# Linear attention with top-1 experts on one core: state sums, tables, a weight load and three copies in another order

## The chip, the core and the metric

One core of a Trainium2 chip runs the whole program. Its engines are TensorE (PE, with PEld for its weight loads), VectorE (DVE), ScalarE (ACT), GpSimd (POOL) and SyncE (SP, which issues most transfers). The metric is the device time of one execution in microseconds. Three timed runs of the kernel before gave 348.38, 348.40 and 348.96 us, median 348.4.

## The reference

```python
# attention: B, H, S, D = 4, 8, 768, 48
for t in range(S):
    state = alpha[:, :, t, :, None] * state + einsum('bhd,bhe->bhde', k[:, :, t], v[:, :, t])
    y[:, :, t] = einsum('bhd,bhde->bhe', q[:, :, t], state)
x = y.transpose(0, 2, 1, 3).reshape(B * S, H * D)          # 3072 rows of 384
# experts: E = 8, F = 1024
logits = x @ w_gate + modality_bias[modality_id]
e_idx = argmax(logits, axis=1)
gate_w = softmax(logits)[arange(N), e_idx]
for e in range(E):
    mask = e_idx == e
    out[mask] = gate_w[mask, None] * (maximum(x[mask] @ w1[e], 0) @ w2[e])
```

## The kernel before, in words

**Attention.** The four batches make two groups of two, and each sequence six chunks of 128 tokens, so there are 12 pairs (`PS`), numbered 0 to 11; pair s holds 256 rows of x. A loop over steps s works as a pipeline: step s scans alpha for the pairs s and s+1, computes scores and outputs of pair s-1, and turns, stores and routes pair s-2. For each pair and each half z of its heads (z0, z1), DVE scans alpha backwards (`G`, in `back`) and forwards (`Fw`, in `forth`); the keys are scaled by G on POOL (`kh`), the queries by Fw on DVE or POOL (`qh`). PE makes the scores from kh and qh, ACT copies them out (`scT`), POOL sets the acausal half to zero, PE multiplies with v. The state is carried from pair to pair: PE sums keys times values in the PSUM tile `kv` (`states`), DVE adds what came before to S (`state`: `S<-UB,kv`), POOL scales S by the decay (`decayed`: `UB<-S,G`), and PE multiplies the queries with UB at the next step (`from_state`: `b<-qh,UB`). Of every six pairs the first needs no UB.

**Routing.** PE multiplies the outputs with the gate's weights (`logits_turned`, copied to `lts` by ACT) and adds their four parts with `fold` (`add_logits`: `kv<-fold,lts`, in the same PSUM tile as kv). DVE finds the expert of each row (`route_group`, last result `oh`), PE counts, DVE turns counts into ranks and places (`rank_...`, `route_places`, `keys_early`). The sorted rows go in slots of 256 to the experts. The first two slots are chosen early, from the rows known so far: expert number to `meta`, weights by SP (`weights`), rows by two indirect transfers of POOL (`gather`: `xg<-xd,idx`).

**Experts.** From about 120 us PE works through 11 full slots and a half one: layer 1 with w1, layer 2 with w2, each weight split into a high and a low part (`w1H`, `w1L`). The first slot uses w2 as it was loaded (`y<-w2r,hf`).

**What sets the order.** The wrapper `Ordered` keeps PE, DVE, ACT and POOL in the order of the code; `at(s, phase, f)` puts a routing step at a place in the pipeline. A transfer of SP is placed by a scheduler unless `tc.issue_after` ties it to an instruction. Each engine works through its own list, and a waiting instruction holds all behind it.

Of the kernel before, what the change touches and what calls it, by code (L numbers as in the profile page):

```python
# [8 lines left out]
F32 = mybir.dt.float32  # L9
# [3 lines left out]
I32 = mybir.dt.int32  # L13
U32 = mybir.dt.uint32
ALU = mybir.AluOpType
AF = mybir.ActivationFunctionType
AX = mybir.AxisListType
# [4 lines left out]
P = 128  # L22
# [54 lines left out]
def attention_moe(ctx: ExitStack, tc: tile.TileContext, q, k, v, alpha, at_, kt_, qt_, vt_, mid, wg, wgp_, mb, w1, w2, out):  # L77
# [123 lines left out]
    of = cp.tile([P, DM], F32, name="of")  # L201
    pool.memset(of, 0.0)
    ti = ac.tile([P, NU], I32, name="ti")
    pool.iota(ti, [[P, NU]], base=-MID, channel_multiplier=1)
    tok = cp.tile([P, NU], F32, name="tok")
    pool.tensor_copy(tok, ti)
    tge = ac.tile([P, NU], F32, name="tge")
    pool.tensor_scalar(tge, tok, 0.0, None, op0=ALU.is_ge)
    pool.tensor_tensor(tok, tok, tge, op=ALU.add)
    rev = cp.tile([P, E], F32, name="rev")  # L210
    ones = cp.tile([P, P], BF16, name="ones")
    tri = cp.tile([P, P], BF16, name="tri")
# [46 lines left out]
    def scaled_queries(s, z, engine=vec):  # L259
        engine.tensor_tensor(st[s, "q"][:, z], QT[s % NB][:, z], seg(st[s, "F"], 1, z), op=ALU.mult)  # L260
# [49 lines left out]
    def decayed(s):  # L310
        if s % NC > 0:
            A = st[s, "G"][:, 1::SEG].unsqueeze(2).broadcast_to([P, KS, D])
            pool.tensor_tensor(UB[s % 2][:, :, :D], st[s, "S"], A, op=ALU.mult)

    def from_state(s):
        yk = [bank(NP, P) for _ in range(2)]
        st[s, "yp"] = yk
        st[s, "fresh"] = {(z, x) for z in range(2) for x in range(2)}
        if s % NC > 0:
            qh, U = st[s, "q"], UB[s % 2]  # L320
            for j in range(NP):
                for z in range(2):
                    for g in range(2):
                        x = g ^ z
                        k = NP * z + j
                        pe.matmul(yof(yk, z, x, j), U[halves[g], k], qh[halves[g], k], start=new(s, z, x), stop=False)
# [25 lines left out]
    def state(s):  # L352
        if s % NC > 0:
            S1 = sb.tile([P, KS, D], F32, name="S")
            kv = st[s - 1, "kv"]
            if s % NC > 1:
                vec.tensor_tensor(S1, UB[(s - 1) % 2][:, :, :D], kv, op=ALU.add)
            else:
                vec.tensor_copy(S1, kv)
            st[s, "S"] = S1  # L360
# [13 lines left out]
                        stop=(j == NP - 1),  # L374
                    )

    def outputs(s):
        yt = sb.tile([P, 2, NP, P], F32, name="yt")
        for z in range(2):
            act.copy(yt[:, z], st[s, "yp"][z])  # L380
        st[s, "yt"] = yt

    def rows(s):
        xs = sb.tile([P, 2, DM], F32, name="xs")
# [159 lines left out]
    K8 = cp.tile([P, E], F32, name="K8")  # L544
    K16 = cp.tile([P, 2, E], F32, name="K16")
    zi = ac.tile([P, 1], I32, name="zi")
    zc = cp.tile([P, 1], F32, name="zc")
    sz = cp.tile([P, 1], F32, name="sz")
    dz = cp.tile([P, NH], F32, name="dz")

    def counting_tables():
        pool.tensor_scalar(rev, iof[:, :E], -1.0, float(E), op0=ALU.mult, op1=ALU.add)
        pool.memset(ones, 1.0)
        for u in range(2):
            pool.tensor_scalar(thr0[:, u], iof[:, :NS0], float(T), float(P * u), op0=ALU.mult, op1=ALU.add)
        pool.memset(on16, 1.0)
        pool.memset(beg[:, 0:1], 0.0)
        pool.memset(C[:, 0:1], 0.0)
        pool.tensor_scalar(K8, rev, -float(NU), None, op0=ALU.mult)
        pool.memset(dE, 1.0)  # L560
        pool.memset(dE[:, 0:1], 0.0)
        pool.memset(dE[:, E : E + 1], 1.0 - E)

    def token_tables():
        pool.affine_select(tri, ones, [[1, P]], ALU.is_gt, 0.0, base=0, channel_multiplier=-1)
        pool.tensor_copy(tok16, tok)
        pool.iota(zi, [[0, 1]], base=0, channel_multiplier=1)
        pool.tensor_copy(zc, zi)
        pool.tensor_scalar(dz, ident[:, :NH], zc, None, op0=ALU.mult)
# [5 lines left out]
    hi = cp.tile([P, NU], F16, name="hi")  # L575
    OH = cp.tile([P, NU, NH], F16, name="OH")
    def half_index():

        hz = cp.tile([P, NS], F32, name="hz")
        vec.tensor_scalar(hz, iof[:, 1 : NS + 1], 2.0, None, op0=ALU.mult)  # L580
        vec.tensor_scalar(hz, hz, zc, None, op0=ALU.is_le)
        vec.tensor_reduce(sz, hz, axis=AX.X, op=ALU.add)

    def places(tp, z):
        return vec.tensor_scalar(idx[:, z], tp, float(MID), 0.0, op0=ALU.add, op1=ALU.max)
# [279 lines left out]
    def at(s, phase, f, *a):  # L865
        later.setdefault((s, phase), []).append((f, a))

    def run(s, phase):
        for f, a in later.pop((s, phase), ()):
            f(*a)  # L870

    for m in range(NM + 1):
        at(3 + m, "masks", bias_table, m)
    at(6, "end", token_tables)
    at(7, "end", half_index)
    at(7, "end", route_group, 0, 10)
    at(8, "small", rank_counts, 0, 10)
    at(8, "middle", rank_masks, 0, 10)
    at(8, "middle", rank_sums, 0, 10)
    at(8, "end", rank_split, 0, 10)  # L880
    at(9, "middle", route_places, 0, 5)
    at(9, "sums", route_places, 5, 10)
    at(9, "end", route_group, 10, 16)
    at(10, "small", rank_counts, 10, 16)
# [1 line left out]
    at(10, "middle", rank_sums, 10, 16)  # L886
    at(10, "sums", count_early, 0)
    at(10, "sums", choose_early, 0)
    at(10, "end", rank_split, 10, 16)
    at(10, "end", route_places, 10, 16)  # L890
    at(10, "end", keys_early, 0)
    at(11, "small", early_places, 0)
    at(11, "small", gather, 0, row(EARLY[0]))
    at(11, "end", gate_values, 0, EARLY[0])

    ZS = (Z0, Z1)
    MORE, LESS = (4,), (11,)
# [18 lines left out]
    def warm(n):  # L916
        w = bank(NP, P)
        for i in range(n):
            pe.matmul(w[:, i % NP], ident, ident, start=True, stop=True)

    for s in range(PS):
        if 0 < s and s + 1 < PS:
            load(s + 1, "kqv")
        if 0 <= s - 2:
            outputs(s - 2)
        late, by = [], vec
        if s == 0:
            warm(14)
            begin(0)
            for z in ZS:  # L930
                back(0, z)
                scaled_keys(0, z, pool)
                totals(0, z)
                forth(0, z)
                scaled_queries(0, z, vec if z == Z0 else pool)
                if z == Z0:
                    counting_tables()
        elif s == 1:
            begin(1)
            scores(0, 0)  # L940
            for z in range(2):
                turn_keys(0, z)
                warm(4)
            back(1, Z0)
            scaled_keys(1, Z0, pool)
            scores(0, 1)
            totals(1, Z0)
            forth(1, Z0)
            scaled_queries(1, Z0, pool)
            back(1, Z1)  # L950
            scaled_keys(1, Z1, pool)
            totals(1, Z1)
            forth(1, Z1)
            scaled_queries(1, Z1)
        else:
            state(s - 1)
            decayed(s - 1)
            for z in range(2):
                scores(s - 1, z)
            run(s, "masks")  # L960
            todo = scans(s)
            if len(todo) > 1:
                late = todo.pop()
            if s >= 4:
                by = pool
            for f in todo:
                do(f)
            run(s, "counts")
        if 1 < s:
            keys(s - 1)  # L970
        if 0 <= s - 2:
            rows(s - 2)
        if 0 <= 2 * (s - 3) < TURNED:
            turn_logits(s - 3)
        if 0 <= s - 2:
            logits_turned(s - 2)
        run(s, "small")
        if 0 <= 2 * (s - 3) < TURNED:
            sum_logits(s - 3)
        run(s, "middle")  # L980
        do(late[:-1])
        if 0 <= s - 1:
            from_state(s - 1)
        if TURNED <= 2 * (s - 2):
            add_logits(s - 2)
        if 0 <= s - 1:
            states(s - 1)
        run(s, "sums")
        for f, *x in late[-1:]:
            f(*x, by)  # L990
        if 0 <= s - 1:
            from_values(s - 1)
        run(s, "end")
        for c in range(s - (s < 5), s + 1 - (s < 4)):
            if 0 <= c < PS:
                guard(c)
        if 0 <= s - 2:
            store(s - 2)
        for c in range(s + 2 + (s > 4), s + 3 + (s > 3)):
            if c < PS:  # L1000
                load(c, "a")
        if s == 2:
            sp.dma_start(xd[MID : MID + 1], of[0:1])
            sp.dma_start(gd[MID : MID + 1], of[0:1, 0:1])
# [34 lines left out]
    def w1_part(i, j):  # L1039
        return split("w1", WR[i % 2][0][:, :, 256 * j : 256 * (j + 1)])  # L1040
# [18 lines left out]
    t = GROUPS[-2:]  # L1059
    state(l)  # L1060
    decayed(l)
    w1s = [w1_part(0, 0)]
    outputs(l - 1)
    for z in range(2):
        scores(l, z)
    out_of_range()
    rows(l - 1)
    logits_turned(l - 1)
    gate_rows(0, EARLY[0])
    gather_gates(0, row(EARLY[0]))  # L1070
    store(l - 1)
    weights(0, 0, (1,))
    from_state(l)
    add_logits(l - 1)
    prep(0, False)
# [3 lines left out]
    low_inputs(0)  # L1079
    rank_counts(*t[0])  # L1080
    count_early(1)
    choose_early(1)
    rank_masks(*t[0])
    w1s += [w1_part(0, 1)]
    outputs(l)
    hp = first_block(0, w1s[0], lambda: logits_turned(l), True)
    rank_split(*t[0])
    keys_early(1)
    w1s += [w1_part(0, 2)]
    rows(l)  # L1090
    store(l)
# [281 lines left out]
```

## Time and profile before

| | |
|---|---|
| median of three timed runs | 348.4 us |
| profiled execution | 349.39 us, its span 347.7 us |
| busy in the span: PE, PEld, DVE | 334.3, 303.0, 270.5 us |
| busy in the span: ACT, POOL | 229.8, 171.4 us |
| transfers | 76.53 MB, mean 220 GB/s |

The span runs from the first to the last instruction of the core; the execution's own time is 1.7 us longer. Shares of busy time are means over stages: the attention lasts until about 115 us, and the experts until 340 us. A gap on PE in either stage has a name, and the views say what ended it.

### The profile page before, as it was taken

The numbers are of one execution on the slowest core, as the hardware profiler recorded it, in microseconds if no ns is written. First come the engines' busy times: TensorE is split into PE (matmuls) and PEld (weight loads), VectorE is DVE, ScalarE is ACT, GpSimd is POOL, SyncE is SP. The second block draws the span as 40 slices with busy tenths as digits, with TensorE's granted clock in tenths as the row PEclk, the third lists the DMA queues.
The fourth block names the chain that finished last, engine by engine and source line by source line (L and its number), as shares of the span: only waits on it lengthen the run. The fifth ranks groups of instructions, "written<-read, shape, count | busy, mean of one in ns | idle before, by whom it ended". The sixth has DMA issues, their size and how long they took to land. (4 is left out here: it accounts for less than half of the span.)

```text
span 347.7 us, 8429 instructions
## 1 busy us (share of the span) xinstructions
PE 334.3 (96%) x3174; PEld 303.0 (87%) x3174; DVE 270.5 (78%) x486; ACT 229.8 (66%) x454; POOL 171.4 (49%) x185
## 2 busy tenths in 40 slices
PE   8999999999898999999999999999999999999991
PEld 8788888888786886898989898989898989898991
DVE  7999999899995768786868686868686868686530
ACT  1677978767566624777777777777777777777530
POOL 7978898787765225555242424232354342411021
PEclk9999999999999999999999999999999999999998
DMA  7999999999169292997776667667586776770010
GB/s 243 393 303 261 244 244 249 252 248 228 48 207 342 101 353 74 378 380 265 255 244 207 246 210 247 206 226 232 180 268 227 232 247 207 236 216 23 2 48 32
DMA packets 39369, 76.53 MB, mean 220 GB/s; under 512 B 4300, under 2 KB 20837, under 8 KB 39317
## 3 DMA queue, kind: packets, MB, share of 16 engines
q1 hardware_dynamic: 35220, 65.83, 61.1%
q0 software_dynamic: 4096, 10.05, 8.6%
q8 instruction: 27, 0.44, 0.5%
q14 instruction: 26, 0.20, 0.2%
HBM read 66.22 MB, written 9.65 MB: 218 GB/s over the span
## 5 line engine op out<-in xcount | busy, mean ns | idle before, releaser
L67 PE MATMUL b<-xHL,w1H 128*128 128x512 f32 (+1 forms) x312 | 103.2, 381 | 0.0
L67 POOL DMA_INDIRECT out_dram<-os,idx x25 | 27.4, 1096 | 112.2 <-ACT os L67 72.1
L67 PE MATMUL b<-xHL,w1L 128*128 128x256 f32 x288 | 80.7, 281 | 0.0
L67 PEld LDWEIGHTS b<-xHL,w1H 128*128 128x128 f32 x312 | 57.4, 188 | 11.8 <-issue 0.4
L67 PE MATMUL y<-w2H,hH 128*128 128x384 f32 x184 | 62.5, 340 | 0.0
L67 PE MATMUL y<-w2H,hL 128*128 128x384 f32 x184 | 61.6, 335 | 0.0
L67 PE MATMUL y<-w2L,hH 128*128 128x384 f32 x184 | 61.5, 334 | 0.0
L67 DVE TENSOR_TENSOR hs<-b,low 128x256 f32<-128x256 f32 x88 | 33.9, 416 | 32.8 <-ACT low L67 31.3
L67 PEld LDWEIGHTS b<-xHL,w1L 128*128 128x128 f32 x288 | 54.3, 189 | 0.1
L67 DVE TENSOR_TENSOR w1L<-w1r,w1H 128x768 fp32r<-128x768 f32 x48 | 43.9, 952 | 6.6 <-ACT w1H L67 6.6
L67 DVE TENSOR_TENSOR w2L<-w2r,w2H 128x768 fp32r<-128x768 f32 x48 | 45.9, 961 | 3.4 <-ACT w2H L67 3.1
L67 ACT ACTIVATE os<-y,gg 128x384 f32<-128x384 f32 x25 | 14.6, 582 | 39.9 <-PE y L67 39.9
L67 ACT COPY low<-b 128x256 f32<-128x256 f32 x88 | 30.4, 367 | 14.8 <-PE b L67 14.6
L67 ACT CAST w2H<-w2r 128x768 fp32r<-128x768 f32 x48 | 40.0, 841 | 0.0
L67 ACT CAST w1H<-w1r 128x768 fp32r<-128x768 f32 x48 | 37.9, 838 | 2.3 <-POOL kh L67 2.3
L67 POOL DMA_INDIRECT gg<-gd,idx x26 | 29.1, 1120 | 19.6 <-issue 13.3
L67 POOL DMA_INDIRECT xg<-xd,idx x26 | 27.6, 1061 | 19.3 <-DVE idx L67 9.8
L67 PEld LDWEIGHTS y<-w2L,hH 128*128 128x128 f32 x184 | 34.6, 188 | 0.0
L67 PEld LDWEIGHTS y<-w2H,hH 128*128 128x128 f32 x184 | 34.6, 188 | 0.0
L67 PEld LDWEIGHTS y<-w2H,hL 128*128 128x128 f32 x184 | 34.5, 188 | 0.0
L67 ACT COPY scT<-b 128x512 f32<-128x512 f32 x48 | 24.9, 598 | 14.2 <-PE b L67 14.0
L67 POOL TENSOR_TENSOR kh<-kt,G 128x512 f32<-128x512 f32 x24 | 31.7, 1328 | 5.2 <-DVE G L67 2.1
(176 smaller groups left out, 605.2 us busy)
## 6 DMA issues: line engine op xcount, KB each, us to landing
w1r<-in_w_dram SPq DMA_DIRECT2D x26, 768.0 KB
w2r<-in_w_dram SPq DMA_DIRECT2D x26, 768.0 KB
vt<-in_paired_v_dram SPq DMA_DIRECT2D x12, 384.0 KB
xd<-xs SPq DMA_DIRECT2D x12, 384.0 KB
X<-in_turned_alpha_dram SPq DMA_DIRECT2D x18, 193.7 KB
kt<-in_turned_k_dram SPq DMA_DIRECT2D x18, 192.0 KB
qt<-in_turned_q_dram SPq DMA_DIRECT2D x18, 192.0 KB
kt<-in_turned_k_dram SPq DMA_DIRECT2D x4, 256.0 KB
```

The lines of the kernel that those rows point to most:

```text
L67: ins = f(*a, **kw)
```

## The change

Five things are done together.

- **State sums.** `state` of pair 9 runs in step 9 ahead of `route_places` and `route_group`, that of pair 10 in step 10 ahead of `rank_split`. In the last step, the gate's values (`gate_values`) come behind `state` and `decayed`. In the steps that start a sequence, `states` stands ahead of `add_logits`.
- **Transfers.** The load of the first slot's w2 is tied to the store of pair 10 (the last but one of the twelve).
- **Start.** The first query products change engines: z0 goes to POOL, z1 to DVE. Of eight filler matmuls (`warm`) in step 1 two stay.
- **Tables.** Constant tables on POOL move: the counting tables ahead of the first kh, the token tables to the end of step 8, the slot tables to the last step; `half_index` is two DVE instructions in place of three, and later.
- **Output copy.** One of the last pair's two copies on ACT (`yt`) goes ahead of a cast of w1.

On VectorE, in steps 9 and 10, around the routing of tiles 10 to 15: before,

```order
L67 SCALAR_TENSOR_TENSOR Fw<-X_87,room 128x516
L67 TENSOR_TENSOR OL<-ioh,lo 128x640
L67 TENSOR_TENSOR L<-kv,bt 128x48
L67 TENSOR_REDUCE mx<-L 128x6
L67 TENSOR_TENSOR ls<-L,mx 128x48
L67 SCALAR_TENSOR_TENSOR eq<-ls,rev 128x48
L67 TENSOR_REDUCE m_176<-eq 128x6
L67 TENSOR_TENSOR oh<-eq,m_176 128x48
L67 TENSOR_TENSOR S<-UB_138,kv 128x384
```

and of the change:

```order
L67 SCALAR_TENSOR_TENSOR Fw<-X_87,room 128x516
L67 TENSOR_TENSOR S<-UB_138,kv 128x384
L67 TENSOR_TENSOR OL<-ioh,lo 128x640
L67 TENSOR_TENSOR L<-kv,bt 128x48
L67 TENSOR_REDUCE mx<-L 128x6
L67 TENSOR_TENSOR ls<-L,mx 128x48
L67 SCALAR_TENSOR_TENSOR eq<-ls,rev 128x48
L67 TENSOR_REDUCE m_172<-eq 128x6
L67 TENSOR_TENSOR oh<-eq,m_172 128x48
```

The state sum S of pair 9 moves past seven routing instructions; oh, which PE counts, now stands behind it.

On SyncE's queue, from the first slot's w1 (`w1r_92`) on, with `xd<-xs` the stores of rows and `gd<-gs` the store of gates: before,

```order
L67 DMA w1r_92<-in_w_dram 128x3x512
L67 DMA xd<-xs 128x2x384
L67 TENSOR_LOAD meta
L67 ISA x3
L67 DMA w2r_93<-in_w_dram 128x4x384
L67 ISA
L67 DMA w2r_93<-in_w_dram 128x4x384
L67 DMA xd<-xs 128x2x384
L67 DMA gd<-gs_16_1942 16x128
L67 DMA xd<-xs 128x2x384
```

and of the change:

```order
L67 DMA w1r_92<-in_w_dram 128x3x512
L67 DMA xd<-xs 128x2x384 x2
L67 DMA gd<-gs_16_1932 16x128
L67 DMA xd<-xs 128x2x384
L67 TENSOR_LOAD meta
L67 ISA x3
L67 DMA w2r_93<-in_w_dram 128x4x384
L67 ISA
L67 DMA w2r_93<-in_w_dram 128x4x384
```

Both halves of w2 (`w2r_93`) now stand behind the stores of pairs 9 and 10 and the gates.

On GpSimd at the start, around the key products kh of pair 0: before,

```order
L67 TENSOR_SCALAR tge<-tok 128x24
L67 TENSOR_TENSOR tok<-tok,tge 128x24
L67 TENSOR_TENSOR kh<-kt_82,G 128x512
L67 TENSOR_SCALAR rev<-iof 128x8
L67 MEMSET ones 128x128
L67 TENSOR_SCALAR thr_199<-iof 128x12 x2
L67 MEMSET dE 128x16
L67 MEMSET dE 128x1 x2
L67 TENSOR_TENSOR kh<-kt_82,G 128x512
L67 TENSOR_TENSOR qh<-qt_84,Fw 128x512
```

and of the change:

```order
L67 TENSOR_SCALAR K_202<-rev 128x8
L67 MEMSET dE 128x16
L67 MEMSET dE 128x1 x2
L67 TENSOR_TENSOR kh<-kt_82,G 128x512
L67 TENSOR_TENSOR qh<-qt_84,Fw 128x512
L67 TENSOR_TENSOR kh<-kt_82,G 128x512
L67 AFFINE_SELECT scT<-scT 128x1024
```

POOL now has qh of z0 between the two kh, the tables stand ahead of both, and qh of z1 is gone from POOL.

The diff, without the moved table lines that repeat:

```diff
-    pool.iota(ti, [[P, NU]], base=-MID, channel_multiplier=1)
-    pool.tensor_copy(tok, ti)
-    pool.tensor_scalar(tge, tok, 0.0, None, op0=ALU.is_ge)
-    pool.tensor_tensor(tok, tok, tge, op=ALU.add)
...
-    def outputs(s):
+    def outputs(s, zs=(0, 1)):
...
-    def counting_tables():
-        pool.tensor_scalar(rev, iof[:, :E], -1.0, float(E), op0=ALU.mult, op1=ALU.add)
...
+    pool.tensor_scalar(rev, iof[:, :E], -1.0, float(E), op0=ALU.mult, op1=ALU.add)
+    pool.memset(ones, 1.0)
...
+    def order_table():
+        pool.affine_select(tri, ones, [[1, P]], ALU.is_gt, 0.0, base=0, channel_multiplier=-1)
+
+    def token_table():
+        pool.iota(ti, [[P, NU]], base=-MID, channel_multiplier=1)
+        pool.tensor_copy(tok, ti)
+        pool.tensor_scalar(tge, tok, 0.0, None, op0=ALU.is_ge)
+        pool.tensor_tensor(tok, tok, tge, op=ALU.add)
+        pool.tensor_copy(tok16, tok)
...
+    def slot_tables():
         for u in range(2):
             pool.tensor_scalar(thr0[:, u], iof[:, :NS0], float(T), float(P * u), op0=ALU.mult, op1=ALU.add)
...
-        vec.tensor_scalar(hz, iof[:, 1 : NS + 1], 2.0, None, op0=ALU.mult)
-        vec.tensor_scalar(hz, hz, zc, None, op0=ALU.is_le)
-        vec.tensor_reduce(sz, hz, axis=AX.X, op=ALU.add)
+        with nc.allow_low_precision("whole numbers"):
+            vec.tensor_scalar(zh, zi, 1, None, op0=ALU.arith_shift_right)
+        vec.tensor_scalar(sz, zh, float(NS), None, op0=ALU.min)
...
-    at(6, "end", token_tables)
-    at(7, "end", half_index)
+    at(6, "end", order_table)
+    at(8, "end", token_table)
...
+    at(9, "sums", state, 9)
     at(9, "sums", route_places, 5, 10)
...
+    at(10, "end", state, 10)
     at(10, "end", rank_split, 10, 16)
...
-    at(11, "end", gate_values, 0, EARLY[0])
...
-                scaled_queries(0, z, vec if z == Z0 else pool)
-                if z == Z0:
-                    counting_tables()
+                scaled_queries(0, z, pool if z == Z0 else vec)
...
-                warm(4)
+                if z == 0:
+                    warm(2)
...
-            state(s - 1)
+            if (s - 1, "S") not in st:
+                state(s - 1)
             decayed(s - 1)
+            run(s, "state")
...
+        if 0 <= s - 1 and (s - 1) % NC == 0:
+            states(s - 1)
         if TURNED <= 2 * (s - 2):
             add_logits(s - 2)
-        if 0 <= s - 1:
+        if 0 <= s - 1 and (s - 1) % NC:
             states(s - 1)
...
+    gate_values(0, EARLY[0])
     w1s = [w1_part(0, 0)]
...
+    slot_tables()
     out_of_range()
...
     store(l - 1)
-    weights(0, 0, (1,))
+    with tc.issue_after(sp.last):
+        weights(0, 0, (1,))
...
     count_early(1)
+    outputs(l, (0,))
     choose_early(1)
     rank_masks(*t[0])
     w1s += [w1_part(0, 1)]
-    outputs(l)
+    outputs(l, (1,))
...
     keys_early(1)
+    half_index()
```

## Rows read from the trace of the kernel before

**Rows 1.** Windows: engines' busy time, PEclk, DMA share, GB/s; and page part 2, PE

```profile
24.00:56.00 32.00, 32.00 (x572) 27.82 (x570) 31.09 (x41) 26.01 (x57) 27.35 (x28) 1.00 0.99 251
56.00:104.00 48.00, 45.78 (x801) 40.17 (x799) 45.76 (x83) 32.68 (x74) 36.12 (x35) 1.00 0.79 204
104.00:120.00 16.00, 14.35 (x189) 11.85 (x184) 9.72 (x39) 9.94 (x21) 7.29 (x7) 1.00 0.57 206
120.00:340.00 220.00, 220.00 (x1341) 203.43 (x1340) 163.07 (x297) 148.45 (x281) 78.84 (x72) 1.00 0.65 217
PE   8999999999898999999999999999999999999991
```

**Rows 2.** Waits of PE in 0 to 140 us: us in total, times, longest

```profile
PE b L67 <- POOL UB L67: 1.2, 2, 0.9
PE b L67 <- DMA xg<-xd,idx: 0.9, 2, 0.6
PE kv L67 <- ACT lts L67: 0.6, 1, 0.6
PE b L67 <- ACT yt L67: 0.6, 1, 0.6
...
PE b L67 <- DVE ohs L67: 0.3, 1, 0.3
```

**Rows 3.** Timeline of the start: start, duration, engine, operation, idle before and releaser

```profile
1.42 5.85 PE L67 MATMUL b<-ident 128*128 128x128 f32 x28 [1.42 <-POOL ident masks.py:199]
...
6.34 0.69 DVE L67 TENSOR_TENSOR qh<-qt,Fw 128x512 f32<-128x512 f32 x1
...
7.19 1.23 DVE L67 TENSOR_TENSOR_SCAN G<-X,room 128x516 f32<-128x516 f32 x1 [0.15 <-DMA X<-in_turned_alpha_dram]
...
9.98 1.19 POOL L67 TENSOR_TENSOR qh<-qt,Fw 128x512 f32<-128x512 f32 x1 [0.29 <-DVE Fw L67]
...
15.21 1.14 DVE L67 TENSOR_TENSOR qh<-qt,Fw 128x512 f32<-128x512 f32 x1
...
17.45 1.16 PE L67 MATMUL b<-qh,kh 48*128 48x128 f32 x16 [0.43 <-POOL kh L67]
```

**Rows 4.** Timeline of PE in step 7

```profile
62.69 0.61 PE L67 MATMUL kv<-fold,lts 128*128 128x8 f32 x4 [0.64 <-ACT lts L67]
63.23 1.14 PE L67 MATMUL kv<-vt,knat 128*64 128x48 f32 x32
```

**Rows 5.** Timeline of DVE at the end of step 7

```profile
64.39 1.12 DVE L67 TENSOR_SCALAR hz<-iof 128x19 f32<-128x19 f32 x1
65.62 1.03 DVE L67 TENSOR_SCALAR hz<-hz,zc 128x19 f32<-128x19 f32 x1
```

**Rows 6.** Timeline around the state of pair 9

```profile
88.27 0.21 DVE L67 TENSOR_TENSOR oh<-eq,m 128x48 bf16<-128x48 f32 x1
...
89.02 0.84 POOL L67 TENSOR_TENSOR UB<-S,G 128x384 f32<-128x384 f32 x1 [1.33 <-DVE S L67]
...
89.91 1.10 PE L67 MATMUL b<-qh,UB 64*64 64x128 f32 x32 [0.92 <-POOL UB L67]
```

**Rows 7.** Timeline around the state of pair 10

```profile
98.78 0.55 DVE L67 TENSOR_TENSOR S<-UB,kv 128x384 f32<-128x384 f32 x1
```

**Rows 8.** Timeline of w2's load, its first use and the gather; DMA queues, 104 to 108

```profile
99.57 1.09 SPq L67 DMA_DIRECT2D w2r<-in_w_dram  x2
...
104.11 1.26 POOL L67 DMA_INDIRECT xg<-xd,idx  x1 [0.17 <-DVE sm L67]
...
127.18 3.39 PE L67 MATMUL y<-w2r,hf 128*128 128x384 f32 x10
...
q1 hardware_dynamic: 1035, 1.54, 104.2%
```

**Rows 9.** Timeline of ACT, the last pair's second output copy

```profile
115.95 0.58 ACT L67 COPY yt<-b 128x512 f32<-128x512 f32 x1 [1.42 <-PE b L67]
```

**Rows 10.** Windows: the span's end

```profile
344.60:347.60 3.00, 0.00 (x0) 0.00 (x0) 0.00 (x0) 0.00 (x0) 0.00 (x0) 0.50 0.02 5
```

More of the change, by code (lines that the diff above doesn't have):

```diff
@@ L375, in from_values @@
                     )
-    def outputs(s):
[L378 to L381, printed above, removed]
+    def outputs(s, zs=(0, 1)):
+        if 0 in zs:
+            st[s, "yt"] = sb.tile([P, 2, NP, P], F32, name="yt")
+        for z in zs:
+            act.copy(st[s, "yt"][:, z], st[s, "yp"][z])
     def rows(s):
@@ L546, in attention_moe @@
     zi = ac.tile([P, 1], I32, name="zi")
+    zh = ac.tile([P, 1], I32, name="zh")
     zc = cp.tile([P, 1], F32, name="zc")
@@ L549, in attention_moe @@
     dz = cp.tile([P, NH], F32, name="dz")
-    def counting_tables():
-        pool.tensor_scalar(rev, iof[:, :E], -1.0, float(E), op0=ALU.mult, op1=ALU.add)
-        pool.memset(ones, 1.0)
+    pool.tensor_scalar(rev, iof[:, :E], -1.0, float(E), op0=ALU.mult, op1=ALU.add)
+    pool.memset(ones, 1.0)
+    pool.memset(on16, 1.0)
+    pool.memset(beg[:, 0:1], 0.0)
+    pool.memset(C[:, 0:1], 0.0)
+    pool.tensor_scalar(K8, rev, -float(NU), None, op0=ALU.mult)
+    pool.memset(dE, 1.0)
+    pool.memset(dE[:, 0:1], 0.0)
+    pool.memset(dE[:, E : E + 1], 1.0 - E)
+    def order_table():
[7 more added lines that the diff above has]
+    def slot_tables():
         for u in range(2):
             pool.tensor_scalar(thr0[:, u], iof[:, :NS0], float(T), float(P * u), op0=ALU.mult, op1=ALU.add)
[L556 to L566, printed above, removed]
         pool.iota(zi, [[0, 1]], base=0, channel_multiplier=1)
@@ L577, in half_index @@
     def half_index():
-        hz = cp.tile([P, NS], F32, name="hz")
-        vec.tensor_scalar(hz, iof[:, 1 : NS + 1], 2.0, None, op0=ALU.mult)
-        vec.tensor_scalar(hz, hz, zc, None, op0=ALU.is_le)
-        vec.tensor_reduce(sz, hz, axis=AX.X, op=ALU.add)
+        with nc.allow_low_precision("whole numbers"):
+            vec.tensor_scalar(zh, zi, 1, None, op0=ALU.arith_shift_right)
+        vec.tensor_scalar(sz, zh, float(NS), None, op0=ALU.min)
     def places(tp, z):
```

## The prediction

> **What bounds the kernel now.** I read the windows first: a table of each engine's busy time by stage. From 120 to 340 us PE is busy for 220.00 of 220 us, and from 24 to 56 us for all of 32 [rows 1]. So the end moves one for one with the moment at which PE enters the experts, as long as no new gap opens behind it. Between them PE is idle for 48 - 45.78 = 2.22 us (56 to 104) and 16 - 14.35 = 1.65 us (104 to 120), 3.87 us together [rows 1]. The waits of PE name nearly all of it: 1.2 us in two waits for UB, 0.9 in two for the gathered rows xg, 0.6 for lts, 0.6 for yt, 0.3 for ohs [rows 2]. The reader is to see a sharp bound: closing every gap behind 24 us gives 3.87 us, and only the start can give more. The second thing to see is DVE, busy for 45.76 of 48 us in the same stage [rows 1]: what is moved there has little room, so its list must be counted through, not only PE's.
>
> Then I read the timelines at each gap, to see which instruction the releaser itself had waited for.
>
> **The change part by part.**
>
> *Step 7, states ahead of add_logits.* PE waits 0.64 us for the copy lts, and then sums keys times values for 1.14 us [rows 4]. Put first, those 1.14 us cover the copy. Removed 0.64; bounds 0 (if the keys' copy for them were as late) and 0.64; I take 0.64, since the copy of the keys stands ahead of lts on ACT.
>
> *half_index.* Two DVE instructions of 1.12 and 1.03 us go from the end of step 7 [rows 5]; two small ones come behind 118 us, beside PE's first block of the first slot. PE gains nothing directly, but DVE is 2.15 us ahead from 64.4 us on. That pays for what follows.
>
> *S of pair 9 ahead of the routing.* Before, S follows oh on DVE, UB had left POOL idle for 1.33 us until S came, and PE waited 0.92 us for UB [rows 6]. Now S comes before the routing instructions. POOL is free 1.33 us before 89.02, at 87.69, and UB (0.84) would be ready by 88.5, in time for PE at 88.99. PE by then comes 0.84 us earlier (0.64 and 0.2 from the start, below), at 88.15, but POOL's work hangs on DVE, which is 2.15 ahead. The price: oh now stands behind S and comes 0.55 later (the same operation as in [rows 7]), 88.48 + 0.55 - 2.15 = 86.9, where PE counts it just ahead of 88.99 - 0.84 = 88.15. Removed 0.92; without DVE's lead about 0.1. I take 0.92. The next wait, 0.3 for ohs [rows 2], is in the same list on DVE: bounds 0 and 0.3; PE is then 1.8 ahead and DVE 2.15, so it is near even, and I take half, 0.17.
>
> *S of pair 10.* It ends at 99.33 behind the whole of rank_split, route_places and keys_early [rows 7], and UB after it makes PE wait for the rest of the 1.2 us, 0.3 [rows 2]. Moved ahead, that is gone; the places that PE counts with come 0.55 later on a DVE that is 2.15 ahead. Removed 0.33, bounds -0.4 and 0.33.
>
> *w2 behind the store of pair 10.* SP issues w2 at 99.57, POOL the gather at 104.11; in the 4 us from 104 on, all transfers that ran were of SP's queue, at 104.2% of 16 engines, and none was the gather's [rows 8]. PE waits for xg twice, 0.31 and 0.63 us, 0.9 in all [rows 2]. With 1.57 MB of w2 taken away ahead of it the gather meets only w1 (issued earlier by DVE's lead) and two stores, and it is itself issued about 3 us earlier, since its places come from DVE. PE wants it about 2.3 us earlier. Removed 0.94; bounds 0 and 0.94; I take all. What w2 loses: it is now issued behind the last store but one, which I put near 107 (the rows of pair 10 are turned while PE passes the scores of pair 11, ahead of xg), and first used at 127.18 less my gain, about 123.7 [rows 8]; 16 us for a load that has had 27.6. Behind it on SP stands the second slot's w1, which waits for the second choice of DVE, some microseconds later: nobody waits for SP there.
>
> The Trainium skill, page "DMA: Bandwidth & Descriptors", section "Queues, rings and completion order", says that a transfer engine goes round between the queues that have work, a packet from each. By that rule the gather, on POOL's queue, would not have stood behind w2 but shared with it, and taking w2 away frees little; the row of 104 to 108 us, without one packet of the gather, does not look like sharing, but it cannot tell whether the gather's descriptors were there. The sum by this rule is the second rival's.
>
> *One yt copy ahead of a cast.* PE waits 0.56 us for the last pair's yt [rows 2]. The second of its copies starts at 115.95, having waited 1.42 us for PE and not for the cast [rows 9]. If that late release is PE's own, the moved first copy gives nothing; if it comes from the order on ACT, all. Bounds 0 and 0.56; I take half, 0.28.
>
> *The start.* PE starts pair 1's second scores at 17.45, after 0.43 us of waiting [rows 3]; from 24 us on it is gapless, so this moment counts. On DVE, qh of z0 (0.69) goes, but the scan G of z1 waits for its alpha until 7.19 all the same [rows 3]: DVE stands idle instead. G, reciprocal and Fw end at 9.9 as before; then qh of z1 runs on DVE, 0.69 to 1.14 us [rows 3], and ends at 10.6 to 11.0, against 9.98 + 1.19 = 11.17 on POOL. That is 0.2 to 0.5 us for the second scores. But DVE now enters pair 1 later by this product, 0.7 to 1.1 us, and pair 1's products hang on both engines. On POOL, small table instructions replace others ahead of the first kh; nothing there, as kh waits for the first G too. The six fillers lie in waits. Bounds: 1.0 gained (the waits up to 17.45 vanish) and 0.6 lost (DVE's delay passes through); I take 0.2 gained, nearest to the second scores' row.
>
> *The other tables.* The token table now stands on POOL ahead of UB of pair 8; POOL waits for S there, as it does a step later [rows 6]. The slot tables come behind the last masks, where POOL waits. Nothing for either.
>
> *Sum.* 0.2 + 0.64 + 0.92 + 0.17 + 0.33 + 0.94 + 0.28 = 3.48 us. The profiled execution has a span of 347.7 and a time of 349.39, 1.0 over the median 348.4 of the timed runs. I subtract from the span, 344.2, and by the same distance from the median: **344.9 us**.
>
> **The rivals.**
>
> *DVE takes PE's place.* The two hz instructions, 1.12 and 1.03 us on 19 elements [rows 5], were slow because they stood behind POOL's kh; then the routing that follows may stand behind the same kh, and DVE gains 0.5, not 2.15. Against it: that routing is mostly of other operations. Then oh is late (88.48 + 0.55 - 0.5), PE gains 0.5 up to there instead of 1.9, still 0.33 and 0.94 behind it and half of yt: about 2.0, 346.4 us. 13 in 100.
>
> *The gather is slow of itself.* It is issued 3 us earlier but lands as long after its issue as before; PE, 2.3 us earlier, waits on for 0.9 - 0.7 to 0.9 - 0.3, say 0.5: 345.4 us. 15 in 100.
>
> *The start loses.* DVE's delay in pair 1 passes through, 0.6 lost instead of 0.2 won: 345.7 us. 8 in 100.
>
> *Nothing comes through.* Another chain, such as the second slot's weights, ends each gap anew: 348.4 us. 4 in 100.
>
> *Slower: the clock falls.* Six fillers fewer leave PE idle at 10 to 15 us. PE's granted clock reads 0.50 at the span's end, 1.2 GHz, after PE had been idle from about 340 us; in the attention it stays at 1.00, 2.4 GHz [rows 1, 10], through idle times of up to 0.92 us [rows 6]. If it fell at 9 us, PE's work in the second slice of 8.7 us, at least nine tenths busy [rows 1], would take up to 7 us more, and the climb back, 5.85 us of matmuls at the start [rows 3], at half rate 2.9 more: near 354 us. [...] The Trainium skill, page "TensorE: Matmul & The Clock Gate", section "What's actually happening", says that the slow clock is the default and that activity lifts it, which speaks against taking fillers away; the trace agrees for the end of the span, and shows no fall inside it. 3 in 100.
>
> **How the numbers follow.** My forecast has 57 in 100, its own range is 343.9 to 345.9: all terms in full and a quick start on one side, no half terms on the other. The first three rivals are inside 343.9 to 346.9, which I give. What a measurement can tell from no change is about 0.2%, 0.7 us. Faster by more: the forecast and the first three rivals, 93, less 3 for several coming together: 0.90. Within: 0.04. Slower: the clock, 3, and 3 for a wait that I don't see: 0.06.
>
> **What would show it.** PE idle under 0.6 us from 56 to 104, no wait of PE for UB or lts; oh of tiles 10 to 15 no later than PE's counting; xg landed before PE turns it, at about 107; w2's issue near 107 and no wait before y<-w2r; experts still gapless. It is wrong if PE waits for oh or ohs for more than half a microsecond, if the gather still ends a wait of PE, if PE at 24 us stands later than before, or if PEclk falls under 1.00 before the end.

## The result, and the profile after

The changed kernel is slower: median 352.28 us (348.36 to 354.28, 22 runs) against 348.99 for the kernel before in the same runs, ratio 1.0066, 95% interval 1.0043 to 1.0089 (352.28/348.99 is 1.0094; the ratio leaves out the seven slowest of the 22 runs, from 353.72 us on, whose granted clocks, 0.984 to 0.987, lie among those of the others). 344.9 was forecast. The profiled execution took 353.38 us with a span of 351.6, 3.9 more than the span before.

Windows of the kernel after: PE's busy time first, then PEld, DVE, ACT, POOL, and the granted clock third from the end [rows 1]:

```profile
56.00:104.00 48.00, 43.32 (x729) 37.60 (x725) 46.03 (x75) 32.34 (x71) 35.46 (x35) 0.98 0.74 201
102.40:109.20 6.80, 6.80 (x88) 6.40 (x80) 4.61 (x10) 1.84 (x4) 4.30 (x4) 0.50 0.68 224
104.00:120.00 16.00, 16.00 (x220) 13.87 (x220) 8.54 (x27) 7.85 (x16) 8.39 (x12) 0.84 0.47 152
120.00:340.00 220.00, 219.92 (x1343) 203.16 (x1342) 164.32 (x314) 151.00 (x285) 80.57 (x72) 1.00 0.66 219
```

Idle time of PE between 56 and 104 us rose from 2.22 to 4.68 us, and from 102.40 to 109.20 us its clock is at half, 1.2 GHz. From 104 to 120 us it has no gap left, where it had 1.65 us; the experts stay gapless but for 0.08 us. PE's waits in 0 to 120 us, answering to [rows 2]:

```profile
PE b L67 <- DVE oh L67: 2.0, 1, 2.0
PE b L67 <- ACT junk L67: 1.9, 1, 1.9
...
PE b L67 <- DVE ohs L67: 0.8, 1, 0.8
```

The waits for UB, lts, xg and yt, which the forecast wanted removed, are gone; the one for ohs, of which it wanted half removed, grew from 0.3 to 0.8 us. Two new waits stand beside it, and all three are for DVE's routing (the one put down to ACT's junk, long done, is for OHE, the last operand of DVE that those products read). On PE's timeline they are followed by slow work:

```profile
89.11 0.20 PE L67 MATMUL b<-oh,tri 128*128 128x48 bf16 x1 [1.99 <-DVE oh L67]
...
92.86 0.18 PE L67 MATMUL b<-ohs,ones 128*128 128x8 bf16 x1 [0.76 <-DVE ohs L67]
...
101.32 0.55 PE L67 MATMUL b<-OHE,OL 128*128 128x2 f16 x16 [1.93 <-ACT junk L67]
101.81 1.48 PE L67 MATMUL b<-qh,UB 64*64 64x128 f32 x32
103.21 1.02 PE L67 MATMUL kv<-fold,lts 128*128 128x8 f32 x4
104.16 1.95 PE L67 MATMUL kv<-vt,knat 128*64 128x48 f32 x32
105.91 3.55 PE L67 MATMUL b<-scT,vt 128*64 128x128 f32 x32
```

The sums of keys times values took 1.14 us before [rows 4], here 1.95; those of scores times values took 1.93 us before, here 3.55:

```profile
102.85 1.93 PE L67 MATMUL b<-scT,vt 128*64 128x128 f32 x32
```

With qh,UB (1.10 before) and fold (0.61 before) that is 3.2 us. Why the routing is late is seen on DVE and POOL, in order of time around pair 9's S (compare [rows 6]):

```profile
84.11 0.53 DVE L67 TENSOR_TENSOR S<-UB,kv 128x384 f32<-128x384 f32 x1
84.55 1.63 DVE L67 TENSOR_TENSOR OL<-ioh,lo 128x640 f16<-128x640 f16 x1
...
85.46 1.43 POOL L67 TENSOR_TENSOR UB<-S,G 128x384 f32<-128x384 f32 x1
...
86.58 0.38 DVE L67 TENSOR_TENSOR ls<-L,mx 128x48 f32<-128x48 f32 x1
86.84 2.15 POOL L67 TENSOR_SCALAR_AFFINE_SELECT scT<-scT 128x1024 f32<-128x1024 f32 x2
86.99 1.01 DVE L67 SCALAR_TENSOR_TENSOR eq<-ls,rev 128x48 f32<-128x48 f32 x1
88.03 0.20 DVE L67 TENSOR_REDUCE m<-eq 128x6 f32<-128x48 f32 x1
88.27 0.79 DVE L67 TENSOR_TENSOR oh<-eq,m 128x48 bf16<-128x48 f32 x1
```

and around pair 10's S:

```profile
96.05 0.53 DVE L67 TENSOR_TENSOR S<-UB,kv 128x384 f32<-128x384 f32 x1
...
96.69 0.86 POOL L67 TENSOR_TENSOR UB<-S,G 128x384 f32<-128x384 f32 x1
96.72 0.85 DVE L67 TENSOR_SCALAR hr<-r 128x6 int32<-128x6 int32 x1
...
97.49 2.96 POOL L67 TENSOR_SCALAR_AFFINE_SELECT scT<-scT 128x1024 f32<-128x1024 f32 x2
97.61 1.01 DVE L67 SCALAR_TENSOR_TENSOR hi<-m,hr 128x6 f16<-128x6 f32 x1
...
99.41 1.06 DVE L67 TENSOR_SCALAR taken<-rest,base 128x8 f32<-128x8 f32 x1
```

Before, the same instructions of DVE read:

```profile
85.84 0.80 DVE L67 TENSOR_TENSOR OL<-ioh,lo 128x640 f16<-128x640 f16 x1
...
87.78 0.21 DVE L67 SCALAR_TENSOR_TENSOR eq<-ls,rev 128x48 f32<-128x48 f32 x1
...
96.36 0.50 DVE L67 TENSOR_SCALAR hr<-r 128x6 int32<-128x6 int32 x1
...
96.89 0.17 DVE L67 SCALAR_TENSOR_TENSOR hi<-m,hr 128x6 f16<-128x6 f32 x1
...
97.84 0.22 DVE L67 TENSOR_SCALAR taken<-rest,base 128x8 f32<-128x8 f32 x1
```

S itself lasts 0.53 us and comes when it should. But POOL, which before stood idle for 1.33 us until S came [rows 6], now has S early and starts UB and the two masks in the middle of the routing. oh takes 0.79 us instead of 0.21 [rows 6], eq 1.01 instead of 0.21, and hr, hi and taken 0.85, 1.01 and 1.06 instead of 0.50, 0.17 and 0.22. Each of these long ones ends within 0.1 us after an instruction of POOL that it lay beside: the two masks of the first row end at 87.93 and 88.99 us, eq at 88.00 and oh at 89.06. OL is longer too, 1.63 us for 0.80, but beside another instruction: it now starts behind POOL's qh (84.32 to 85.50 us), where before it started ahead of it (qh from 86.06).

### The profile page after: what moved, and what is told of

Same layout as the page of the kernel before. It is cut to its first block, busy times and chain, and to the rows that moved or that the text cites. A ratio compares the mean times of both kernels' runs of the same rounds, so it can differ in the third digit from the quotient of the medians.

```text
span 351.6 us, 8400 instructions
## 1 busy us (share of the span) xinstructions
PE 336.2 (96%) x3162; PEld 305.0 (87%) x3162; DVE 272.3 (77%) x485; ACT 230.5 (66%) x454; POOL 174.0 (49%) x185
## 5 line engine op out<-in xcount | busy, mean ns | idle before, releaser
L67 POOL DMA_INDIRECT out_dram<-os,idx x25 | 26.6, 1062 | 109.5 <-ACT os L67 69.6
L67 POOL DMA_INDIRECT xg<-xd,idx x26 | 32.8, 1260 | 18.1 <-DVE idx L67 8.0
L67 POOL DMA_INDIRECT gg<-gd,idx x26 | 28.0, 1078 | 19.1 <-issue 13.3
L67 POOL TENSOR_TENSOR kh<-kt,G 128x512 f32<-128x512 f32 x24 | 30.5, 1276 | 10.4 <-PE b L67 5.4
```

The lines of the kernel that those rows point to most:

```text
L67: ins = f(*a, **kw)
```

## The experiments

**The port theory:** instructions of DVE and POOL that lie side by side hold each other up; the early S puts POOL's UB and masks beside the routing, oh, ohs and OHE come late, and PE's idle time lets its clock fall. **Rivals:** S's own 0.55 us in front of the routing is the cost; or the clock falls because of the six missing fillers at the start. Every ratio is to the kernel before, timed together with the run.

**The two moves undone, together and one by one, and done alone**

```diff
-    at(9, "sums", state, 9)
-    at(10, "end", state, 10)
```

Both lines go from the changed kernel:

> The change without its two moves of S (states 9 and 10 come at the head of steps 10 and 11 again), all else as changed. Port theory (S early lets POOL's UB product and masks run beside DVE's routing, and the two engines hold each other up): no wait of PE for oh, for the places or for ohs over 0.4 us, the waits for UB are back (about 0.9 and 0.3 us), the granted clock stays at 1.00 up to the end of the last slot, and what the start (1.0), step 7 (0.64), the gathered rows (0.9) and yt (0.3 to 0.56) give comes through: 2.8 to 3.1 us under the kernel before, ratio 0.991 to 0.992. Theory of S alone (only its two times 0.55 us on DVE cost): about 1.1 us under the changed kernel, so still slower than before by about 1 us, ratio 1.003. Start theory (the missing fillers let the clock fall): the granted clock falls near 102 us here too, and the ratio stays near 1.007.

Only the second goes:

> The change with S of pair 9 moved and S of pair 10 where it was. Port theory: in the routing of tiles 10 to 15 the OL, eq and oh instructions are stretched as in the changed kernel, PE waits some 2 us for oh and under 1 us for ohs; the places of the early slot come without a long wait, the wait for UB of pair 10 (0.3 us) is back. With 2.8 us of idle instead of 4.7 the granted clock may hold: then about 346.5 to 347.5 us (ratio 0.994 to 0.997), and if it falls all the same, about 350. Theory of S alone: 0.55 us more than without both moves, ratio about 1.001 and no stretched instruction.

Only the first goes:

> The change with S of pair 10 moved and S of pair 9 where it was. Port theory: oh in time, the UB wait of 0.9 us as before; hr, hi, taken and OHE of the early slot are stretched beside the masks of pair 10, and PE waits 1 to 2 us for the places near 99 us. Granted clock likely 1.00 throughout: about 346.5 to 347.5 us (ratio 0.994 to 0.997). Theory of S alone: 0.55 us more than without both moves.

Both are put into the kernel before (with a test that keeps `state` from running twice):

> The kernel before with nothing but the two moves of S. Port theory: PE waits for oh (1.5 to 2.5 us) and for the places of the early slot (about 2 us) in place of UB, the same DVE instructions are stretched as in the changed kernel, and since DVE is without the 2.15 us that the shorter half_index gives, the waits are no smaller; with the fall of the granted clock 351 to 354 us (ratio 1.008 to 1.015), without it about 349.5 to 351. Theory of S alone: PE saves 1.2 us at UB and pays 1.1 for S: no change, ratio 1.000. Start theory: all fillers are there, so the clock does not fall.

Measured: without the moves 347.45 us, 0.9945 (0.9920 to 0.9971), less gain than I expected; pair 9 alone 1.0006 (0.9983 to 1.0029); pair 10 alone 1.0027 (0.9999 to 1.0055); the moves alone on the kernel before 352.05 us, 1.0076 (1.0047 to 1.0104), with 349.57 for the kernel before in all four. So two lines turn a gain of 2.1 us into a loss. PE's waits from 56 to 120 us without the moves are these, and its clock stays at 1.00 to the last slot:

```profile
PE b L67 <- POOL UB L67: 0.7, 2, 0.4
PE b L67 <- DVE ohs L67: 0.3, 1, 0.3
PE b L67 <- ACT yt L67: 0.2, 1, 0.2
```

With pair 9 alone PE waits 2.0 us for oh and 0.8 for ohs and the clock holds, in a profiled execution of 348.07 us, one of the fastest of 347.92 to 351.49; I had the time lower by 0.3 to 0.6%. With pair 10 alone it waits 1.0 us for UB, 0.3 for ohs and 1.9 for OHE, and the clock falls at 101.73 us, which I had thought unlikely. With the moves on the kernel before PE waits 1.2 us for oh (I had expected at least 1.5), 0.8 for ohs and 1.9 for OHE; all fillers are there, and the clock falls at 102.60 us: the start theory is out. S's own time cannot make waits of 2 us from 0.55, but the next run tests it directly.

**POOL held back, S still early**

UB of pairs 9 and 10 waits for DVE's last instruction of the step, oh or OHE, which `hold` names:

```diff
             pool.tensor_tensor(UB[s % 2][:, :, :D], st[s, "S"], A, op=ALU.mult)
+            if s in (9, 10):
+                tc.add_manual_dep(pool.last, st["hold", s].name, ...)
...
         run(s, "end")
+        st["hold", s] = vec.last
```

> The changed kernel with both early S, but POOL's UB product of pair 9 waits for the last routing instruction of DVE (oh), and that of pair 10 for the last one of the early choice (OHE); the masks behind them on POOL come later by the same. S still stands in front of the routing. Port theory (what costs is POOL's work beside DVE's): eq and oh are short again (0.2 to 0.3 us, not 0.8 to 1.0), PE waits for oh and the places by under 0.5 us each and for UB by about 0.3, the granted clock stays at 1.00, and the time is that without the moves, ratio 0.993 to 0.996. Theory of S alone (what costs is S's 0.55 us ahead of the routing): PE waits on for oh and the places about as in the changed kernel, and the ratio stays above 1.002.

Measured: 347.14 us, 0.9927 (0.9901 to 0.9953). DVE and POOL of this kernel at the same places:

```profile
84.50 0.53 DVE L67 TENSOR_TENSOR S<-UB,kv 128x384 f32<-128x384 f32 x1
84.95 1.64 DVE L67 TENSOR_TENSOR OL<-ioh,lo 128x640 f16<-128x640 f16 x1
...
87.22 0.21 DVE L67 SCALAR_TENSOR_TENSOR eq<-ls,rev 128x48 f32<-128x48 f32 x1
...
87.70 0.21 DVE L67 TENSOR_TENSOR oh<-eq,m 128x48 bf16<-128x48 f32 x1
...
87.99 0.84 POOL L67 TENSOR_TENSOR UB<-S,G 128x384 f32<-128x384 f32 x1 [2.08 <-DVE oh L67]
...
95.12 0.53 DVE L67 TENSOR_TENSOR S<-UB,kv 128x384 f32<-128x384 f32 x1
...
95.80 0.17 DVE L67 TENSOR_SCALAR hr<-r 128x6 int32<-128x6 int32 x1
...
96.00 0.17 DVE L67 SCALAR_TENSOR_TENSOR hi<-m,hr 128x6 f16<-128x6 f32 x1
...
96.95 0.23 DVE L67 TENSOR_SCALAR taken<-rest,base 128x8 f32<-128x8 f32 x1
```

DVE's list is the changed kernel's, word for word, S in front included. Only POOL is out of the way, and eq falls from 1.01 to 0.21 us, oh from 0.79 to 0.21, hr from 0.85 to 0.17, hi from 1.01 to 0.17, taken from 1.06 to 0.23. The theory of S alone is out as the cause of the loss. It is not nothing, though: OL stays at 1.64 us, since S in front of it still lets POOL's qh (84.72 to 85.91) start first; without the moves OL starts at 84.39, ahead of qh at 84.61, and takes 0.80. This reaches no wait of PE here: PE waits 0.6 us for UB, which is held behind oh, and 0.3 for ohs. The time is 2.2 us under the kernel before; against the kernel without the moves (0.9945) the intervals overlap, so no gain of the early S itself is shown.

**Which of POOL's instructions**

```diff
         pool.affine_select(sc, sc, ...)
+        if s in (9, 10) and z == 0:
+            tc.add_manual_dep(pool.last, st["hold", s].name, ...)
```

> The changed kernel with both early S, where UB of pairs 9 and 10 runs on POOL as soon as S is there, but the masks of these pairs wait for oh and OHE on DVE. If the masks are what holds eq and oh, hr, hi and taken up, these take 0.17 to 0.25 us and the time is that with POOL held, ratio 0.992 to 0.995. If the product UB holds them up as well, OL of tiles 5 to 9 and one of hr and hi stay long (0.8 to 1.6 us), oh and the places come 0.5 to 1 us late, ratio 0.995 to 0.999.

Measured: 348.44 us against 349.19, 0.9954 (0.9923 to 0.9985). DVE in this kernel:

```profile
87.98 0.21 DVE L67 SCALAR_TENSOR_TENSOR eq<-ls,rev 128x48 f32<-128x48 f32 x1
...
88.46 0.21 DVE L67 TENSOR_TENSOR oh<-eq,m 128x48 bf16<-128x48 f32 x1
...
96.97 0.85 DVE L67 TENSOR_SCALAR hr<-r 128x6 int32<-128x6 int32 x1
...
97.85 0.17 DVE L67 SCALAR_TENSOR_TENSOR hi<-m,hr 128x6 f16<-128x6 f32 x1
```

Both do it, each to what lies beside it: with the masks held, eq, oh and hi are short, and hr, beside UB, is still 0.85 us. The second expectation fits; the interval reaches into the range of the first.

**The clock by itself**

```diff
+    def fill(t, n):
+        for i in range(n):
+            pe.matmul(t[:, 384:], ident, ident, start=True, stop=True)
```

called with 8 ahead of the products with oh, 3 ahead of ohs, 8 ahead of OHE, in columns of the bank that these use anyway.

> The changed kernel with products of the unit matrix, whose results nobody reads, ahead of the three late waits of PE: 8 before oh, 3 before ohs, 8 before OHE, some 4.1 us of work (0.21 to 0.22 us each in the start) in 4.7 us of waits. If the idle PE is what lets the clock fall, the granted clock stays at 1.00 and the 3.2 us of slow work go: 349 us, ratio 0.998 to 1.001, with the waits on DVE as they were. If the clock falls for another reason (the missing fillers at the start), it falls near 102 us here too and the ratio is 1.007 or more.

Measured: 350.6 us against 349.3, 1.0026 (0.9995 to 1.0057). The windows of this kernel:

```profile
56.00:104.00 48.00, 47.81 (x778) 41.96 (x773) 46.50 (x75) 32.80 (x71) 35.57 (x36) 1.00 0.71 195
104.00:120.00 16.00, 16.00 (x241) 13.93 (x241) 14.29 (x46) 10.00 (x21) 9.28 (x13) 1.00 0.66 213
```

Nothing is won on DVE (eq takes 1.01 us again), yet the clock stays at 1.00 and the span falls from 351.6 to 347.6 us in the two profiled executions; by the ratios the fillers win 0.4%. So work in PE's idle time is enough to keep the clock up. The rest of the loss, 0.3% and not clear of noise, I put down to the waits. The time is above the 0.998 to 1.001 that I expected.

**w2 behind the store of pair 10, taken back**

```diff
-    with tc.issue_after(sp.last):
-        weights(0, 0, (1,))
+    weights(0, 0, (1,))
```

from the kernel without the S moves:

> The kernel without the S moves, and w2 of the first slot no longer behind the store of pair 10. By the prediction's term the waits for the gathered rows xg come back: 0.9 us slower than without the S moves alone, ratio about 0.997. If the gather shares the transfer engines with w2 and is not delayed by it: no difference, ratio 0.9945, and xg lands as soon after its issue.

Measured: 349.89 us, 1.0003 (0.9977 to 1.0030), against 0.9945 with the tie. PE's wait, and the gather's line among the DMA issues of 100 to 116 us (the last number is from issue to landing):

```profile
PE b L67 <- DMA xg<-xd,idx: 1.7, 2, 1.3
```

```profile
xg<-xd,idx POOLq DMA_INDIRECT x2, 6.8
```

With the tie PE does not wait for xg, neither in the kernel without the S moves nor with POOL held, and in the latter the same line reads

```profile
xg<-xd,idx POOLq DMA_INDIRECT x2, 3.7
```

The tie had a term of 0.94 us. By the ratios it is worth 2.0 us, give or take 1.3; by the wait 1.7. (In the trace without the tie PE is 1.1 us later than with it at 60 us already, which the tie cannot have caused.)

How the queues share is less clear. Without the tie the gather is issued at 103.17 us, and the first packet of its queue (q0) runs near 107.7, 4.5 us later; from 103 to 107.5 us 1178 packets of SP's queue (q1) ran, at 104.8% of 16 engines, and none of the gather's. With the tie the first packet comes near 104.6, 1.9 us after the issue at 102.68. From 107.7 us on both queues move side by side. That later stretch agrees with the round-robin of the Trainium skill (page "DMA: Bandwidth & Descriptors", section "Queues, rings and completion order"), the earlier one does not look like it, and no trace shows when the gather's descriptors were there. My rival that the gather is slow of itself did not hold: it lands after 3.7 us without w2 and after 6.8 beside it.

**The shorter half_index taken back**, in the kernel with POOL held, again as two instructions on 19 elements (hz) and a sum:

```diff
+    at(6, "end", slot_tables)
+    at(7, "end", half_index)
...
```

> The kernel with POOL held, but half_index in its old form of two instructions on 19 elements and a sum at the end of step 7 (and the tables it reads in step 6). Prediction's term: the shorter form puts DVE 2.15 us ahead from 64.4 us on; if all of it reaches oh, then here oh comes 2 us later, PE waits for it and for UB 1.5 us or more, and the ratio is 0.997 or above. If the lead melts on the way to the routing of tiles 10 to 15 (DVE's eq and oh of tiles 0 to 9 already stood beside POOL's products in the changed kernel), at most 0.5 us slower than with POOL held, ratio 0.993 to 0.994.

Measured: 348.97 us against 349.44, 0.9977 (0.9943 to 1.0012), where 0.9927 has the short one. From 84 to 120 us PE waits 0.6 us for UB, as with POOL held, and new for

```profile
PE b L67 <- DVE oh L67: 1.4, 1, 1.4
```

So DVE's lead does reach oh, though the two ratios are hardly apart. It is smaller than the 2.15 us of the two hz: from the start of step 7's last Fw to that of S DVE takes 5.54 us here and 3.99 with the short form, 1.55 less, since in the short form two of the routing's instructions, L and ls, lie beside POOL's products (0.90 us each; alone they take 0.23).

**The start**

```diff
-                scaled_queries(0, z, pool if z == Z0 else vec)
+                scaled_queries(0, z, vec if z == Z0 else pool)
-                if z == 0:
-                    warm(2)
+                warm(4)
```

Both edits on the kernel without the S moves:

> The kernel without the S moves, with the first query products on the engines of before and the eight fillers of before (the tables stay moved). By the prediction's term 0.2 us slower than without the S moves alone; by the trace of the changed kernel, where PE began the scores of pair 1's second half 1.0 us sooner, 0.4 to 1.0 us slower, ratio 0.996 to 0.9975. If the start is worth nothing in the median: ratio 0.9945.

Both on the kernel with POOL held:

> Both S early, POOL held behind oh and OHE as in the kernel with POOL held, and the start of before (first query products on the engines of before, eight fillers). If the new start is worth the 0.26 to 1.0 us that the traces with it showed at 25 us, 0.3 to 1.0 us slower than with POOL held and the new start (ratio 0.994 to 0.9955); if it is worth nothing in the median, since the alpha and the queries of pair 2 come no earlier, ratio 0.992 to 0.9935; if it loses, as the last call's run without S moves hints, 0.990 to 0.992, and this is the fastest of all.

The fillers alone on the kernel with POOL held:

> Both S early, POOL held behind oh and OHE, the new first query products, and all eight fillers of before. If the missing fillers cost (the clock fell at 9.93 us in the run of before with the new start), 0.991 to 0.9925 and the least spread of all; if they cost nothing here, as with POOL held, 0.9927; if the fillers stand in PE's way, 0.3 to 0.6 us more, 0.994.

The new start put into the kernel before, with its counting tables ahead of the first keys' product, and then again with the thresholds and the token table put off to step 6:

```diff
-                scaled_queries(0, z, vec if z == Z0 else pool)
-                if z == Z0:
-                    counting_tables()
+                scaled_queries(0, z, pool if z == Z0 else vec)
-                warm(4)
+                if z == 0:
+                    warm(2)
```

> The kernel before with the new start alone: the first query products swapped, six fillers fewer, the counting tables ahead of the first keys' product. Prediction's term: 0.2 us faster, ratio 0.9994 (bounds of the prediction 0.997 to 1.002). If the traces' 0.26 to 1.0 us hold in the median: 0.997 to 0.999. If the loads of pair 2 decide: 1.000, PE at 25 us standing up to 0.7 us later in some runs. The granted clock stays at 1.00 from the start to the last slot if the missing fillers do no harm.

> The kernel before with the new start, now with the thresholds and the token table out of the way of the first keys' product (in the last such run they put it off from 4.80 to 6.30 us); these tables come in step 6. Prediction's term: 0.9994, bounds 0.997 to 1.002. If the late keys' product was what cost in that run: 0.997 to 1.000, the first keys' product at about 4.9 us and a granted clock of 1.00 from there to the last slot. If the swap and the missing fillers lose by themselves: 1.002 to 1.005, with a fall of the clock near 10 us in the profile.

Measured: 346.27 us, 0.9916 (0.9883 to 0.9949); 347.39 us, 0.9951 (0.9921 to 0.9981); 347.34 us, 0.9946 (0.9923 to 0.9969); on the kernel before 1.0033 (0.9996 to 1.0070) and 1.0035 (0.9997 to 1.0073). The first says that the new start loses 0.3%, the second that it wins 0.2%; both intervals overlap those of their partners. The last two don't measure the start alone: in the one the tables put off the first keys' product from 4.80 to 6.30 us, in the other the tables in step 6 made PE wait 1.5 us for scT near 64 us. In both the clock falls for some 3 us between 112 and 118 us, after PE waited 1.08 and 0.32 us for xg in the one, 1.28 and 0.34 in the other, whose window reads

```profile
104.00:120.00 16.00, 14.38 (x198) 11.92 (x194) 11.30 (x28) 7.87 (x17) 8.58 (x8) 0.89 0.60 219
```

In the medians the start stays open, between 1.2 us lost and 0.8 won. The traces show which part moves PE: with all eight fillers it starts pair 1's second scores at 17.65 us with the new engines and at 17.45 to 18.08 with the old ones, with two fillers at 16.90 (POOL held). The six fillers did not lie in waits. And with the late product, the window of the start reads

```profile
9.90:13.40 3.50, 3.50 (x22) 3.17 (x23) 3.36 (x5) 2.11 (x4) 2.26 (x2) 0.51 1.05 394
```

so the clock can fall there too, after PE had waited 1.4 us for the first qh, the fall that my slower rival described.

## Why the prediction was wrong

**The failed step is "S of pair 9 ahead of the routing", and the same in pair 10.** I priced S at its 0.55 us and let DVE's lead pay, "88.48 + 0.55 - 2.15 = 86.9". oh ended at 89.06. DVE did have the lead: S began at 84.11, and OL after it at 84.55 stood 1.29 us ahead of its place before, 85.84. Then OL, ls, eq and oh together lost 1.87 us beside POOL (0.83 - 0.34 + 0.80 + 0.58), and 1.87 - 1.29 = 0.58 is the lateness. In step 10 S, hr, hi and taken add 0.46 + 0.35 + 0.84 + 0.84 = 2.49 us, and OHE ended at 101.27 instead of 98.86. Holding POOL back, with S left where it is, takes ls, eq and oh back to 0.21 us, hr, hi and taken to 0.17, 0.17 and 0.23, and PE's waits for oh and OHE go: shown. OL's 0.83 us stays; that is S's own, which lets POOL's qh start ahead of OL, and my 0.55 left it out.

What I missed stood in the rows. That UB had "left POOL idle for 1.33 us until S came" I read as a loss; it was what kept the routing's last instructions, eq, m and oh, free of POOL. And I had named the mechanism, in the first rival, for hz behind kh, without asking what else the early S would set going; the kernel before shows it in the routing too, where ls takes 0.72 us and hr 0.50 beside POOL's qh. The Trainium skill, page "SBUF — State Buffer", section "Who interferes with whom", states it: DVE and GpSimd share a pair of ports, locked for a whole instruction; a DVE instruction with two inputs in SBUF, and a copy or tensor_scalar in its fast forms, contends, a reduction never does. The traces agree: OL, ls, eq, oh, hi (two inputs) and hr, taken (tensor_scalar) are the stretched ones, while mx and m keep 0.20 us beside UB and the masks. That it is a port that they share, no run here shows.

**The second failure is the clock.** I gave its fall 3 in 100 and tied it to the fillers missing at the start; it came near 102 us, after three waits of 1.99, 0.76 and 1.93 us, and with all fillers in place as well. The fall cost 3.2 us of slow work. My price for it was built on another place, and its climb back of 5.85 us is not in [rows 3]: the granted clock is 1.00 there from the first microsecond on. The Trainium skill's rule that activity lifts the clock (page "TensorE: Matmul & The Clock Gate", section "What's actually happening") agrees with the fillers' run. The runs of the changed kernel lie 6 us apart, 348.36 us at a mean clock of 0.995, 351 to 354 at 0.981 to 0.989; this may be the same fall, but only one of them has a trace.

Term by term otherwise: step 7 (0.64): in the run without S moves and with the old start the products of scores and values behind it come 0.55 us sooner than before, those ahead of it at the same time; right. half_index (2.15 ahead): too large. From the start of step 7's last Fw to that of S DVE takes 4.41 us instead of 5.66, 1.25 less (1.62 without the S moves), since eq and oh of tiles 0 to 9 now take 1.10 and 1.14 us beside POOL's products, where they took 0.24: the first rival's mechanism, in part. It is worth 0.5% in the end. w2 and xg (0.94): right and too small. w2's issue, put near 107 us, came at 115.36, since the stores it stands behind were late (that of the gates was issued at 113.77), and still no wait for w2 followed. yt (half of 0.56): 0.2 us of the wait is left without the S moves and none in the changed kernel; right. The start (0.2): PE's second scores of pair 1 came at 16.45, 1.0 us sooner than [rows 3], and the scan G that I had wait for its alpha until 7.19 began at 6.24; the six fillers, which I had put in waits, were in PE's way. In medians nothing can be told. The forecast without its S terms and ohs is 0.2 + 0.64 + 0.94 + 0.28 = 2.06 us; the kernel without the S moves measured 349.57 - 347.45 = 2.12. That these agree so well is luck in part: the tie gave more than its term, and the start is open.

Where the 3.9 us of span come from, by PE's timeline against that of before: ahead of pair 9's scores it is 1.58 us early (1.0 from the start, 0.58 from step 7). Then come +2.05 at oh, -0.98 at UB, +0.42 at ohs, +2.00 at OHE, -0.39 at UB and +3.16 of slow work: 4.67 us late at pair 11's scores (109.38 against 104.71). Of these 1.30 come back at the gathered rows, 0.64 at yt and some 0.5 ahead of them: 2.25 us late in the first slot, close to the measured loss of 0.66%, 2.3 us. The slots add another 0.85 us and the end behind the last product 0.8, for which I have no cause.

## What to carry to other kernels

Before you move an instruction forward, ask whom it releases, and what that engine's work will then lie beside: on this chip DVE and POOL can hold each other up for whole instructions, and an idle stretch of POOL may be what keeps a critical run of small DVE instructions short. If the early result is wanted anyway, hold the released work back to the end of that run; here that turned +0.7% into -0.7%, which is no more than leaving the moves out gave (-0.55%, the intervals overlap). And price a wait of TensorE on top of its length with the clock it may cost, here 3.2 us for one fall.

## What was not expected of the hardware

The clock fell with no idle time of PE over 2 us: before the fall it had waited 1.99, 0.76 and 1.93 us in the changed kernel, 1.0, 0.3 and 1.9 us with pair 10 alone. After 2.0, 0.8 and 0.3 us, with pair 9 alone, it stayed at 1.00. The lengths of the waits do not settle it: after 1.28 and 0.34 us for xg it fell in the kernel before with the new start and its tables in step 6, after 1.29 and 0.38 without the tie it stayed. An instruction of 48 elements per partition, 0.21 us long, took 1.01 us beside a POOL instruction of 1.09, so its price is set by its neighbour and not by its size.
